# Attention with a threshold, then a mixture of experts: splitting tau - max behind its transposition

## The chip, the cores and the metric

The kernel runs on one core of one Trainium2 chip, in a single launch. The metric is the device time of that core in microseconds. In this document PE is TensorE's matmul row and PEld its weight loads, DVE is VectorE, ACT is ScalarE, POOL is GpSimd and SP is SyncE, whose queue issues most of the DMAs.

## The reference, cut to what matters

```python
# q, k, v: [8 batches, 8 heads, 576, 64] f32, tau = 0.02
scores = q @ k.T / 8
thresh = max(scores, axis=-1) - tau
scores = where(scores >= thresh, scores, -1e9)
attn   = exp(scores - max(scores)); attn /= sum(attn) + 1e-9
x = (attn @ v)                        # as [4608, 512]
# mixture of experts, top 1 of 8
logits = x @ w_gate; e = argmax(logits); gate = softmax(logits)[e]
out = gate * (relu(x @ w1[e]) @ w2[e])
```

Each row of scores keeps only the entries within tau of its maximum. The kernel must find the maximum first, and only then decide which entries live.

## The kernel before, in words

The 64 heads are taken as 32 pairs. For each pair n the scores are made twice. `s_unit` (L269) makes them with the queries on the partitions, ten units and a corner, and DVE reduces each unit to the negated maximum of its rows (L283, L288), into the tile `nm`: 128 partitions, nine tiles of queries, in two halves (the first 512 keys, the rest). Later `st_unit` (L334) makes them again with the keys on the partitions, ready for the product with v. There the maximum must be known for each column, that is for each query. It is brought in by the matmul itself: rows 64 to 66 of the operand `CQ` hold tau - max of each query, split in three f16 parts, and the same rows of `CK` hold ones, so that the second matmul of a unit (L341) adds tau - max to every score. After it ACT takes the exponential (L357), DVE sets what is below zero to nothing (`mask`, L360), ACT makes the f16 high part of the result (L365) and POOL the low part by a subtraction of two SBUF operands (L366). `av_piece` (L381) multiplies both with v.

`parts` (L290) is what turns `nm` into those three rows. On DVE it takes the smaller of the two negated maxima (L297), adds the threshold and rounds to f16 (L306), takes the remainder (L307), rounds that (L308) and takes what is left (L310). Each of the five works on 9 columns in SBUF and 128 partitions. Three steps later `turn` brings the 27 columns to 27 partitions with one f16 matmul against an identity (L321), ACT copies them from PSUM to SBUF (L326), and three DMAs on SP's queue write them to rows 64 to 66 of `CQ` (L328).

The order is written as steps: 11 steps a pair, in each of which one unit of `s` of a later pair and one of `st` of an earlier one are issued. The scores of pair n are finished 11 steps before its first `st` unit. Work that isn't a unit is put in a table by `plan` and `after` at a step and one of three places in it (FRONT, MID, END), and `chain` lays a list out at two operations a step, MID and END. A scheduler below that orders the instructions of each engine from this.

Between the units go the conversion of q, k and v (L206, L209, L242, L243), the normalisation of a finished batch, its gate (`logits`, `route`, `ranks`), and the scatter of its rows to a buffer by expert (`send`, L550). PSUM is eight banks: five for scores, two for the product with v, and one pool of one bank, `ps_m`, which `parts`, the gate's logits and its ranks share. When the last batch is scattered, the experts run: rows are gathered by expert, transposed by DMA, and go through two matrix products (L793, L820).

Of the kernel before, what the change touches and what calls it, by code (L numbers as in the profile page):

```python
# [9 lines left out]
F16 = mybir.dt.float16  # L10
F32 = mybir.dt.float32
I32 = mybir.dt.int32
U32 = mybir.dt.uint32
AF = mybir.ActivationFunctionType
ALU = mybir.AluOpType
AX = mybir.AxisListType

P = 128
B, H, S, D = 8, 8, 576, 64
# [23 lines left out]
CAP = NTOK  # L43

TUNE = dict(
    lead=10, cast=2, pst=3, sl=8, ll=15, sp0=3, sps=0, lv=-16, sv0=-6, sv1=2, av=2, g=4, l=3, d=4, g5=4, l5=3, d5=2, g6=1, l6=2, d6=2, g7=1, l7=1, d7=1, off=2, off5=1, off6=11, lg=4, lg7=13, km=16, rate=15, dh=1, do=3, ws0=6, wsd=1, w1d=5, plv=1, xv=3, so=0, sto=0, ord=0, sc=5, fa=3, fd=4, wa1=-70, wa2=-86, wl1=-28, wl2=-6, avb=2, route=1, ranks=7, pt2=1, pta=0, pch=0, pp=8, ew=4, maskat=0, w1a=-40, w1b=3,
)


# [1 line left out]
def kernel(  # L51
# [9 lines left out]
    nc = tc.nc  # L61

    cpool = ctx.enter_context(tc.tile_pool(name="cpool", bufs=1))
# [3 lines left out]
    ps_m = ctx.enter_context(tc.tile_pool(name="ps_m", bufs=1, space=bass.MemoryType.PSUM))  # L67
    small = ctx.enter_context(tc.tile_pool(name="small", bufs=3))
    rpool = ctx.enter_context(tc.tile_pool(name="rpool", bufs=1))
    tp = ctx.enter_context(tc.tile_pool(name="tp", bufs=1))  # L70
    ew = ctx.enter_context(tc.tile_pool(name="ew", bufs=4))
# [7 lines left out]
    op = apool.enter_context(tc.tile_pool(name="op", bufs=4))  # L79
    pp = apool.enter_context(tc.tile_pool(name="pp", bufs=8))  # L80


    ident = cpool.tile([P, P], F16, name="ident")
    make_identity(nc, ident)
    ones = cpool.tile([P, P], F16, name="ones")
    nc.gpsimd.memset(ones, 1.0)
# [4 lines left out]
    thr = cpool.tile([P, 1], F32, name="thr")  # L91
# [67 lines left out]
    st = {}  # L159
# [7 lines left out]
    FRONT, MID, END = range(3)  # L167

    def plan(k, f, where=END):
        assert (k, where) >= (now[0], slot[0])  # L170
        acts.setdefault(k, ([], [], []))[where].append(f)

    def after(k, f, where=END):
        plan(now[0] + k, f, where)

    def chain(k, fs):

        for i, f in enumerate(fs):
            i += slot[0] > FRONT and k == 0
            after(k + i // 2, f, END if i % 2 else MID)  # L180
# [108 lines left out]

    def parts(n):  # L290

        nm = st[n]["nm"]
        pt = small.tile([P, 3, 9], F16, tag="pt", name=f"pt_{n}")
        r1 = small.tile([P, 2, 9], F32, tag="r1", name=f"r1_{n}")
        r, x = r1[:, 0], r1[:, 1]
        v, a, g = nc.vector, nc.scalar, nc.gpsimd
        fs = [lambda: v.tensor_tensor(r, nm[:, 0], nm[:, 1], ALU.min)]  # L297
        if TUNE["pta"]:
            fs += [
                lambda: a.activation(pt[:, 0], r, AF.Identity, bias=thr),  # L300
                lambda: v.scalar_tensor_tensor(x, r, thr, pt[:, 0], ALU.add, ALU.subtract),
                lambda: a.copy(pt[:, 1], x),
            ]
        else:
            fs += [
                lambda: v.tensor_scalar(pt[:, 0], r, thr, None, ALU.add),  # L306
                lambda: v.scalar_tensor_tensor(x, r, thr, pt[:, 0], ALU.add, ALU.subtract),  # L307
                lambda: v.tensor_copy(pt[:, 1], x),  # L308
            ]
        fs.append(lambda: (g, v)[TUNE["pt2"]].tensor_tensor(pt[:, 2], x, pt[:, 1], ALU.subtract))  # L310
        if TUNE["pch"]:
            chain(0, fs)
            z = len(fs) // 2
        else:
            for f in fs:
                f()
            z = 0

        def turn():
            pst = ps_m.tile([P, 512], F32, tag="m", name=f"pst_{n}")  # L320
            nc.tensor.matmul(pst[0:27, 0:P], pt.rearrange("p a t -> p (a t)"), ident, start=True, stop=True)  # L321
            after(1, lambda: rows(pst), FRONT)

        def rows(pst):
            ptT = small.tile([27, P], F16, tag="ptT", name=f"ptT_{n}", bufs=2)
            nc.scalar.copy(ptT, pst[0:27, 0:P])  # L326
            for p in range(3):
                nc.sync.dma_start(  # L328
                    st[n]["CQ"][64 + p:65 + p].rearrange("p (t c) -> p t c", t=9), ptT[9 * p:9 * p + 9]
                )  # L330

        after(PST + z, turn)

    def st_unit(n, t):  # L334
        d = st[n]
# [39 lines left out]
    def x_tiles(b):  # L375
        if b not in xt:
            half = xt[b - 1][1] if b % 2 else xp.tile([P, H, W], F32, tag="xh", name=f"xh_{b}")
            xt[b] = (xp.tile([P, NT, H, W], F32, tag="x", name=f"x_{b}"), half)
        return xt[b]
# [49 lines left out]
    def finish(b):  # L429
        x = str(b) if b >= B - 3 else ""  # L430
        gap, lag, dist = (TUNE[z + x] for z in "gld")
        off = TUNE["off" + x] if b < B - 1 else 2
        n = NT + b % 2
        x4, xh = x_tiles(b)
        rs = small.tile([P, 5, H], F32, tag="rs", name=f"rs_{b}")
        eps = 1e-9 * SV / SX
        fs = [
            lambda: nc.vector.tensor_scalar(rs[:, 0:NT].unsqueeze(3), x4[:, :, :, D:W], eps, None, ALU.add),
            lambda: nc.vector.reciprocal(rs[:, 0:NT], rs[:, 0:NT]),
        ]  # L440
        if n > NT:
            fs += [
                lambda: nc.vector.tensor_scalar(rs[:, NT].unsqueeze(2), xh[:, :, D:W], eps, None, ALU.add),
                lambda: nc.vector.reciprocal(rs[:, NT], rs[:, NT]),
            ]
        chain(0, fs)
        xTs = {}

        def one(j):
            xr = x4[:, j] if j < NT else xh  # L450
            x = xp.tile([P, DM], F32, tag="xn", name=f"xn_{b}_{j}", bufs=2).rearrange("p (h d) -> p h d", h=H)
            eng = nc.vector if (b, j) in XV else nc.gpsimd
            eng.tensor_tensor(
                x, xr[:, :, 0:D], rs[:, j].unsqueeze(2).to_broadcast([P, H, D]), ALU.mult
            )
            x = x.rearrange("p (c u) d -> p c (u d)", c=4)
            Rv = R[:, j, 0:DM].bitcast(F16).rearrange("p (c h d) -> p c h d", c=4, h=2)

            def high():
                nc.scalar.copy(Rv[:, :, 0, :], x)  # L460
                eng.tensor_tensor(Rv[:, :, 1, :], x, Rv[:, :, 0, :], ALU.subtract)
                after(lag, turn)

            def turn():
                if j % 2 == 0:
                    xTs["t"] = rpool.tile([P, 2, 8, P], F16, tag="xT", name=f"xTg_{b}_{j}", bufs=3)
                xTs[j] = xT = xTs["t"][:, j % 2]
                nc.sync.dma_start_transpose(xT, R[:, j, 0:DM].bitcast(F16))

            after(lag, high)  # L470

        for j in range(n):
            after(off + gap * j, lambda j=j: one(j))
        after(off + gap * (n - 1) + 2 * lag + TUNE["lg7" if b == B - 1 else "lg"], lambda: logits(b, n, xTs, dist))

    def logits(b, n, xTs, dist):
        lg = ps_m.tile([P, 512], F32, tag="m", name=f"lg_{b}")
        lv = lg[:, 0:n * 2 * E].rearrange("p (j h e) -> p j h e", j=n, h=2)
        seq = [(0, 0)] + [(c, 1) for c in range(4)] + [(c, 0) for c in range(1, 4)]
        for j in range(n):  # L480
            for m, (c, h) in enumerate(seq):
                nc.tensor.matmul(
                    lv[:, j, 0:2 - h], xTs[j][:, 2 * c + h, :], wg[:, c, 0:2 - h, :],
                    start=(m == 0), stop=(m == 7),
                )
        after(1, lambda: nc.vector.tensor_reduce(
            L[:, 0:n, :], lv.rearrange("p j h e -> p j e h"), axis=AX.X, op=ALU.add
        ), FRONT)
        after(TUNE["route"], lambda: route(b, n, dist))
# [362 lines left out]
    NSTEP = len(st_order)  # L852
    av_order = [(a, i) for a in range(2) for i in range(NT)] + [(0, NT), (1, NT)]
    SL, LL = TUNE["sl"], TUNE["ll"]
    LEAD, CAST, PST = TUNE["lead"], TUNE["cast"], TUNE["pst"]
    KEND = NSTEP * NPAIR
    KM = KEND - TUNE["km"]
    NF = 3
# [146 lines left out]
    turn = [8]  # L1005
# [24 lines left out]
    if True:  # L1030
# [9 lines left out]
        while busy:  # L1040
# [3 lines left out]
            for z in (("st", "s"), ("s", "st"))[TUNE["ord"]]:  # L1044
                n, t = divmod(k + (NSTEP + LEAD if z == "s" else 0), NSTEP)
                if z == "s" and n < NPAIR:
                    s_unit(n, s_order[t])
                    if t == NSTEP - 1:
                        parts(n)
                elif z == "st" and 0 <= n < NPAIR:  # L1050
                    masks.append(st_unit(n, st_order[t]))
# [5 lines left out]
            n, t = divmod(k - TUNE["av"], NSTEP)  # L1057
# [94 lines left out]
```

## Time and profile before

| | |
|---|---|
| median of 3 runs | 1158.68 us (1156.25 to 1160.17) |
| the profiled execution | 1160.5 us, span 1158.5 us |
| PE busy | 970.1 us (84%) |
| DVE busy | 865.3 us (75%) |
| ACT busy | 645.4 us (56%) |
| POOL busy | 586.1 us (51%) |

The span runs from the first to the last instruction of the profiled execution. Busy shares over the whole span mix two stages: attention, to about 725 us, and the experts behind it. A row of the groups by line gives the busy time of all instructions of one line and shape, the mean of one, and how long the engine stood idle just before them.

### The profile page before, as it was taken

The numbers are of one execution on the slowest core, as the hardware profiler recorded it, in microseconds if no ns is written. First come the engines' busy times: TensorE is split into PE (matmuls) and PEld (weight loads), VectorE is DVE, ScalarE is ACT, GpSimd is POOL, SyncE is SP. The second block draws the span as 40 slices with busy tenths as digits, with TensorE's granted clock in tenths as the row PEclk, the third lists the DMA queues.
The fourth block names the chain that finished last, engine by engine and source line by source line (L and its number), as shares of the span: only waits on it lengthen the run. The fifth ranks groups of instructions, "written<-read, shape, count | busy, mean of one in ns | idle before, by whom it ended". The sixth has DMA issues, their size and how long they took to land. (4 is left out here: it accounts for less than half of the span.)

```text
span 1158.5 us, 26702 instructions
## 1 busy us (share of the span) xinstructions
PE 970.1 (84%) x10699; PEld 625.8 (54%) x10699; DVE 865.3 (75%) x1449; ACT 645.4 (56%) x998; POOL 586.1 (51%) x459
## 2 busy tenths in 40 slices
PE   4788788688778679778679768988799999999997
PEld 1354454355445345445346436765667667676774
DVE  8899999999999999999999997465242343234460
ACT  2667676677567667667567667342243344334451
POOL 2356764885585776676766686443312222222221
PEclk9889888999889989989989988989799999999999
DMA  6544433354344435345433442797974575666640
GB/s 190 133 139 105 116 75 96 118 115 110 87 115 125 123 82 138 93 108 137 127 62 89 119 116 66 227 246 225 221 220 144 157 208 148 164 200 163 227 135 25
DMA packets 142554, 159.06 MB, mean 137 GB/s; under 512 B 96345, under 2 KB 112731, under 8 KB 142428
## 3 DMA queue, kind: packets, MB, share of 16 engines
q1 hardware_dynamic: 133276, 127.88, 42.6%
q0 software_dynamic: 9152, 29.45, 7.8%
q8 instruction: 85, 1.39, 0.5%
q14 instruction: 41, 0.34, 0.1%
HBM read 90.24 MB, written 19.44 MB: 95 GB/s over the span
## 5 line engine op out<-in xcount | busy, mean ns | idle before, releaser
L366 POOL TENSOR_TENSOR pl<-e,ph 128x1024 f16<-128x1024 f32 x158 | 349.9, 2220 | 206.5 <-ACT ph L365 133.5
L357 ACT ACTIVATE e<-st,ntau 128x512 f32<-128x512 f32 (+1 forms) x352 | 221.4, 651 | 67.7 <-PE st L341 63.7
L360 DVE SCALAR_TENSOR_TENSOR e<-st,e 128x512 f32<-128x512 f32 (+1 forms) x352 | 217.6, 635 | 6.4 <-ACT e L357 6.3
L288 DVE TENSOR_REDUCE nm<-s 128x1 f32<-128x512 f32 x320 | 199.8, 633 | 16.6 <-PE s L278 15.1
L793 PEld LDWEIGHTS <-wb 128*128 128x128 f16 x2304 | 193.6, 100 | 30.8 <-DMA xTm<-R 11.7
L365 ACT CAST ph<-e 128x1024 f16<-128x1024 f32 x160 | 166.7, 1042 | 74.8 <-DVE e L360 74.1
L276 PE MATMUL s<-QK 128*128 128x512 f16 (+3 forms) x640 | 146.9, 306 | 72.5 <-DVE nm L288 41.9
L793 PE MATMUL h<-xTm,wb 128*128 128x256 f16 (+2 forms) x2112 | 197.9, 256 | 11.2 <-DMA xTm<-R 11.2
L820 PE MATMUL y<-wb,hl 128*128 128x512 f16 (+1 forms) x1056 | 203.3, 362 | 3.2 <-ACT hl L781 2.4
L340 PE MATMUL st<-QK 128*128 128x512 f16 (+3 forms) x640 | 147.0, 309 | 61.7 <-DVE nm L288 34.5
L405 PE MATMUL av<-vop,ph 128*128 128x64 f16 (+1 forms) x1280 | 168.6, 200 | 0.0
L407 PE MATMUL av<-vop,ph 128*128 128x65 f16 (+1 forms) x1280 | 168.6, 201 | 0.0
L406 PE MATMUL av<-vop,pl 128*128 128x65 f16 (+1 forms) x1280 | 168.2, 200 | 0.4 <-POOL pl L366 0.4
L712 DVE SCALAR_TENSOR_TENSOR wb<-wf,wb 128x1024 f16<-128x1024 f32 x96 | 121.5, 1301 | 42.6 <-ACT wb L711 41.1
L820 PEld LDWEIGHTS <-hl 128*128 128x128 f16 (+1 forms) x1056 | 94.5, 100 | 103.0 <-issue 4.2
L341 PE MATMUL st<-CQ,ck 128*128 128x512 f16 (+3 forms) x640 | 145.0, 306 | 5.0 <-DMA CQ<-ptT 5.0
L278 PE MATMUL s<-ck,CQ 128*128 128x512 f16 (+3 forms) x640 | 145.9, 303 | 0.0
L406 PEld LDWEIGHTS <-pl 128*128 128x128 f16 (+1 forms) x1280 | 126.9, 105 | 26.7 <-issue 12.9
L407 PEld LDWEIGHTS <-ph 128*128 128x128 f16 (+1 forms) x1280 | 126.8, 105 | 25.0 <-issue 14.2
L405 PEld LDWEIGHTS <-ph 128*128 128x128 f16 (+1 forms) x1280 | 126.9, 105 | 21.6 <-issue 12.2
L751 DVE COPY gt<-R 128x1 f32<-128x1 f32 x35 | 5.4, 154 | 148.3 <-DMA out_dram<-o,gt 127.5
L781 ACT ACTIVATE hl<-h 128x512 f16<-128x512 f32 (+1 forms) x80 | 45.6, 572 | 126.0 <-PE h L793 126.0
(184 smaller groups left out, 1338.4 us busy)
## 6 DMA issues: line engine op xcount, KB each, us to landing
wf<-in_w_dram SPq DMA_DIRECT2D x96, 512.0 KB
qkf<-in_qk_dram SPq DMA_DIRECT2D x32, 576.0 KB
vf<-in_v_dram SPq DMA_DIRECT2D x16, 640.0 KB
QK<-hi SPq DMA_DIRECT2D x64, 144.0 KB
QK<-hi SPq DMA_DIRECT2D x64, 72.0 KB
QK<-lo SPq DMA_DIRECT2D x64, 72.0 KB
ck<-lo SPq DMA_DIRECT2D x64, 72.0 KB
CQ<-hi SPq DMA_DIRECT2D x64, 64.0 KB
```

The lines of the kernel that those rows point to most:

```text
L276: nc.tensor.matmul(sc[rows, oc], d["QA"][a][:, cols], d["KB"][a][:, CH[c]], start=True, stop=False)
L288: nc.vector.tensor_reduce(o, sc[:, 0:width(t)], axis=AX.X, op=ALU.max, negate=True)
L340: nc.tensor.matmul(sc[rows, oc], d["KB"][a][:, cols], d["QA"][a][:, CH[c]], start=True, stop=False)
L357: nc.scalar.activation(pf, sc, AF.Exp, bias=ntau, scale=0.125 / SS)
L360: nc.vector.scalar_tensor_tensor(pf, sc, 0.0, pf, ALU.is_ge, ALU.mult)
L365: nc.scalar.copy(h, pd)
L366: (nc.vector if (n, t) in PLV else nc.gpsimd).tensor_tensor(l, pd, h, ALU.subtract)
L405: nc.tensor.matmul(av[rows, a, 0:D], h, vop[:, tv, W:W + D], start=False, stop=False)
L406: nc.tensor.matmul(av[rows, a], l, vop[:, tv, 0:W], start=False, stop=False)
L407: nc.tensor.matmul(av[rows, a], h, vop[:, tv, 0:W], start=False, stop=a == 1 and i >= 2 and j == NT - 1)
L793: nc.tensor.matmul(o, Wt[:, c, wh, f], x, start=c == 0 and z == 0, stop=c == 3 and z == 2,)
L820: nc.tensor.matmul(o, h[:, hh], Wt[:, f, wh, c], start=f == 0 and z == 0, stop=f == 7 and z == 2)
```

## The change

The five operations on 128 partitions become one: a reduction over the two halves of `nm` into one f32 tile of 9 columns. That tile is transposed as f32, one step later, by a matmul with an f32 identity into the bank of `ps_m`. The split is then made on 9 partitions and 128 columns: ACT reads PSUM, adds the threshold and rounds to f16; DVE writes the remainder to other columns of the same bank; ACT rounds that; DVE subtracts. The four are put by `chain` on two steps. Then the three DMAs are issued. The SBUF tile of the three parts has one buffer instead of two, and the options of `TUNE` for the old split go (`pst`, `pt2`, `pta`, `pch`).

```diff
-    ident = cpool.tile([P, P], F16, name="ident")
+    ident = cpool.tile([P, P], F32, name="ident")
...
-        fs = [lambda: v.tensor_tensor(r, nm[:, 0], nm[:, 1], ALU.min)]
...
-                lambda: v.tensor_scalar(pt[:, 0], r, thr, None, ALU.add),
-                lambda: v.scalar_tensor_tensor(x, r, thr, pt[:, 0], ALU.add, ALU.subtract),
-                lambda: v.tensor_copy(pt[:, 1], x),
...
-        fs.append(lambda: (g, v)[TUNE["pt2"]].tensor_tensor(pt[:, 2], x, pt[:, 1], ALU.subtract))
...
+        r = small.tile([P, 9], F32, tag="r", name=f"r_{n}")
+        nc.vector.tensor_reduce(r, nm.rearrange("p a t -> p t a"), axis=AX.X, op=ALU.min)
         def turn():
-            pst = ps_m.tile([P, 512], F32, tag="m", name=f"pst_{n}")
-            nc.tensor.matmul(pst[0:27, 0:P], pt.rearrange("p a t -> p (a t)"), ident, start=True, stop=True)
-            after(1, lambda: rows(pst), FRONT)
+            ps = ps_m.tile([P, 512], F32, tag="m", name=f"pst_{n}")
+            nc.tensor.transpose(ps[0:9, 0:P], r, ident)
+            x, y = ps[0:9, 0:P], ps[0:9, P:2 * P]
+            t = small.tile([9, 3, P], F16, tag="ptT", name=f"ptT_{n}", bufs=1)
+            v, a = nc.vector, nc.scalar
+            chain(1, [
+                lambda: a.activation(t[:, 0], x, AF.Identity, bias=thr[0:9]),
+                lambda: v.scalar_tensor_tensor(y, x, thr[0:9], t[:, 0], ALU.add, ALU.subtract),
+                lambda: a.copy(t[:, 1], y),
+                lambda: (v.tensor_tensor(t[:, 2], y, t[:, 1], ALU.subtract), rows(t)),
+            ])
-        def rows(pst):
-            ptT = small.tile([27, P], F16, tag="ptT", name=f"ptT_{n}", bufs=2)
-            nc.scalar.copy(ptT, pst[0:27, 0:P])
+        def rows(t):
             for p in range(3):
                 nc.sync.dma_start(
-                    st[n]["CQ"][64 + p:65 + p].rearrange("p (t c) -> p t c", t=9), ptT[9 * p:9 * p + 9]
+                    st[n]["CQ"][64 + p:65 + p].rearrange("p (t c) -> p t c", t=9), t[:, p]
                 )
-        after(PST + z, turn)
+        after(1, turn)
...
-        rs = small.tile([P, 5, H], F32, tag="rs", name=f"rs_{b}")
+        rs = small.tile([P, 5, H], F32, tag="rs", name=f"rs_{b}", bufs=2)
```

## Rows read from the trace of the kernel before

**Rows 1.** Busy time by stretches: us, each engine's busy time (instructions), clock, DMA share, GB/s

```profile
202.90:219.50 16.60, 14.51 (x168) 7.87 (x166) 16.60 (x38) 13.76 (x24) 13.67 (x10) 1.00 0.56 167
50.00:100.00 50.00, 42.83 (x579) 25.90 (x577) 49.55 (x77) 37.92 (x59) 31.16 (x16) 0.93 0.50 136
100.00:700.00 600.00, 468.77 (x6111) 282.98 (x6107) 582.23 (x939) 407.44 (x665) 411.06 (x252) 0.92 0.42 106
28.00:725.00 697.00, 550.98 (x7200) 332.70 (x7199) 668.01 (x1092) 476.40 (x775) 465.09 (x285) 0.91 0.43 108
```

**Rows 2.** Waits of 100 to 700 us: total us, times, longest us

```profile
PE s L276 <- DVE nm L288: 39.2, 39, 5.9
...
ACT ptT L326 <- PE pst L321: 18.1, 9, 4.6
...
DVE nm L288 <- PE s L278: 11.9, 20, 1.7
```

**Rows 3.** Groups by line, DVE, the lines of `parts`: busy us, mean ns, idle before

```profile
L306 DVE TENSOR_SCALAR pt<-r,thr 128x9 f16<-128x9 f32 x32 | 53.4, 1668 | 0.1
...
L297 DVE TENSOR_TENSOR r<-nm 128x9 f32<-128x9 f32 x32 | 27.2, 852 | 0.1
L308 DVE CAST pt<-r 128x9 f16<-128x9 f32 x32 | 22.2, 695 | 0.1
...
L307 DVE SCALAR_TENSOR_TENSOR r<-r,thr,pt 128x9 f32<-128x9 f32 x32 | 18.3, 571 | 0.0
L310 DVE TENSOR_TENSOR pt<-r,pt 128x9 f16<-128x9 f32 x32 | 17.8, 556 | 0.0
```

**Rows 4.** Single lines of DVE: shortest/median/longest ns, first and last start, forms

```profile
L297 DVE TENSOR_TENSOR r<-nm x32: 152/424/5042, 27.9 to 693.4; 128x9 f32<-128x9 f32 x32
...
L310 DVE TENSOR_TENSOR pt<-r,pt x32: 154/158/2117, 35.0 to 699.6; 128x9 f16<-128x9 f32 x32
...
L288 DVE TENSOR_REDUCE nm<-s x320: 208/677/695, 18.1 to 691.9; 128x1 f32<-128x512 f32 x160
...
L360 DVE SCALAR_TENSOR_TENSOR e<-st,e x352: 206/677/693, 42.2 to 722.2; 128x512 f32<-128x512 f32 x156, 128x64 f32<-128x64 f32 x20
...
L533 DVE TENSOR_TENSOR ps<-rk,base_e x8: 175/182/193, 197.5 to 767.1; 128x32 f32<-128x32 f32 x4, 128x40 f32<-128x40 f32 x4
...
L538 DVE TENSOR_REDUCE pos<-ps x8: 169/175/196, 202.9 to 767.5; 128x4 f32<-128x32 f32 x4, 128x5 f32<-128x40 f32 x4
```

**Rows 5.** Timeline of one stall, DVE and POOL: start us, us, instruction

```profile
333.39 7.48 DVE L306 TENSOR_SCALAR pt<-r,thr 128x9 f16<-128x9 f32 x1
333.44 2.14 POOL L366 TENSOR_TENSOR pl<-e,ph 128x1024 f16<-128x1024 f32 x1
335.54 1.15 POOL L461 TENSOR_TENSOR R<-xn,R 128x512 f16<-128x512 f32 x1
336.64 4.19 POOL L366 TENSOR_TENSOR pl<-e,ph 128x1024 f16<-128x1024 f32 x2
```

**Rows 6.** Groups by line and shape, PE

```profile
L341 PE MATMUL st<-CQ,ck 128*128 128x512 f16 x256 | 100.1, 395 | 5.0 <-DMA CQ<-ptT 5.0
...
L321 PE MATMUL pst<-ident,pt 128*27 128x128 f16 x32 | 7.5, 235 | 17.5 <-DVE pt L310 17.2 <-ACT ptT L326 0.3
```

**Rows 7.** Groups by line, DVE, other operations on SBUF alone

```profile
L209 DVE SCALAR_TENSOR_TENSOR lo<-qkf,hi 128x1152 f16<-128x1152 f32 (+1 forms) x33 | 57.4, 1742 | 1.1 <-ACT hi L206 1.1
...
L243 DVE SCALAR_TENSOR_TENSOR vop<-vf,vop 128x640 f16<-128x640 f32 x32 | 30.7, 958 | 0.5 <-ACT vop L242 0.5
...
L511 DVE TENSOR_TENSOR w<-L,mx 128x32 f32<-128x32 f32 (+1 forms) x8 | 8.8, 1100 | 0.1
...
L519 DVE TENSOR_TENSOR oh<-w,mw 128x32 f16<-128x32 f32 (+1 forms) x8 | 4.6, 573 | 0.0
```

**Rows 8.** The chain that ended last, its beginning: start us, us, what

```profile
800.88 0.97 DMA xs<-R,posi
...
808.69 9.06 DMA xTm<-R
817.74 0.05 issue
817.79 8.38 PE h L793 x96
```

More of the change, by code (lines that the diff above doesn't have):

```diff
@@ L45 @@
 TUNE = dict(
-    lead=10, cast=2, pst=3, sl=8, ll=15, sp0=3, sps=0, lv=-16, sv0=-6, sv1=2, av=2, g=4, l=3, d=4, g5=4, l5=3, d5=2, g6=1, l6=2, d6=2, g7=1, l7=1, d7=1, off=2, off5=1, off6=11, lg=4, lg7=13, km=16, rate=15, dh=1, do=3, ws0=6, wsd=1, w1d=5, plv=1, xv=3, so=0, sto=0, ord=0, sc=5, fa=3, fd=4, wa1=-70, wa2=-86, wl1=-28, wl2=-6, avb=2, route=1, ranks=7, pt2=1, pta=0, pch=0, pp=8, ew=4, maskat=0, w1a=-40, w1b=3,
+    lead=10, cast=2, sl=8, ll=15, sp0=3, sps=0, lv=-16, sv0=-6, sv1=2, av=2, g=4, l=3, d=4, g5=4, l5=3, d5=2, g6=1, l6=2, d6=2, g7=1, l7=1, d7=1, off=2, off5=1, off6=11, lg=4, lg7=13, km=16, rate=15, dh=1, do=3, ws0=6, wsd=1, w1d=5, plv=1, xv=3, so=0, sto=0, ord=0, sc=5, fa=3, fd=4, wa1=-70, wa2=-86, wl1=-28, wl2=-6, avb=2, route=1, ranks=7, pp=8, ew=4, maskat=0, w1a=-40, w1b=3,
 )
@@ L292, in parts @@
         nm = st[n]["nm"]
[L293 to L296, printed above, removed]
-        fs = [lambda: v.tensor_tensor(r, nm[:, 0], nm[:, 1], ALU.min)]
-        if TUNE["pta"]:
-            fs += [
-                lambda: a.activation(pt[:, 0], r, AF.Identity, bias=thr),
-                lambda: v.scalar_tensor_tensor(x, r, thr, pt[:, 0], ALU.add, ALU.subtract),
[L302 to L305, printed above, removed]
-                lambda: v.tensor_scalar(pt[:, 0], r, thr, None, ALU.add),
-                lambda: v.scalar_tensor_tensor(x, r, thr, pt[:, 0], ALU.add, ALU.subtract),
-                lambda: v.tensor_copy(pt[:, 1], x),
-            ]
@@ L310, in parts @@
-        fs.append(lambda: (g, v)[TUNE["pt2"]].tensor_tensor(pt[:, 2], x, pt[:, 1], ALU.subtract))
[L311 to L317, printed above, removed]
-        def turn():
-            pst = ps_m.tile([P, 512], F32, tag="m", name=f"pst_{n}")
-            nc.tensor.matmul(pst[0:27, 0:P], pt.rearrange("p a t -> p (a t)"), ident, start=True, stop=True)
-            after(1, lambda: rows(pst), FRONT)
@@ L854 @@
     SL, LL = TUNE["sl"], TUNE["ll"]
-    LEAD, CAST, PST = TUNE["lead"], TUNE["cast"], TUNE["pst"]
+    LEAD, CAST = TUNE["lead"], TUNE["cast"]
     KEND = NSTEP * NPAIR
```

## The prediction

> **What bounds the kernel now.** I read the busy time by stretches first, because the kernel has two stages with different limits. [...] PE stands idle 131 us of the 600, DVE 18.
>
> What does DVE spend it on? The groups by line show five lines of `parts` that are far too dear for 9 columns: 53.4, 27.2, 22.2, 18.3 and 17.8 us for 32 instructions each, 138.9 us together [rows 3]. The spread tells why: the shortest of them take 152 to 222 ns (sum of the five shortest 0.891 us), the longest of the two shown 5.0 and 2.1 us (the first and the last of the five stand in [rows 4]). The reader is to see that the instructions next to them in the same engine don't spread: the reductions and masks that read PSUM lie between 206 and 695 ns over 672 instances, and so does a two-input operation with one operand in PSUM (175 to 193), and a reduction with SBUF on both sides (169 to 196) [rows 4]. What stretches is an operation with SBUF operands alone that is not a reduction.
>
> The timeline shows on what it waits. L306 starts at 333.39 and ends at 340.87; POOL starts a subtraction at 333.44, runs three further ones without a gap, and ends the last at 340.83 [rows 5]. DVE stood until POOL's backlog had run dry. In those 7.4 us no mask was made and no maximum, so PE and ACT ran out as well. Such an operation costs the whole pipeline, not DVE alone.
>
> **The change part by part.** What goes from DVE: five operations per pair, 32 pairs, 138.9 us. Without the stalls they would be 32 x 0.891 = 28.5 us; the stalls are 110.4.
>
> What comes to DVE: one reduction of 18 columns to 9 with SBUF on both sides, 0.175 (L538 in [rows 4]); one three-operand operation on 128 columns with PSUM in and out; one subtraction on 128 columns with one operand in PSUM. For the second I take L360's two shapes: 206 ns at 64 columns, 677 at 512, so 1.05 ns a column, and 0.273 us at 128. For the third, L533's 182 ns at 32 to 40 columns plus some 90 columns gives 0.275. Sum 0.723 x 32 = 23.1 us. Against the 28.5 that is 5 us less, and I count it as nothing, since successive DVE records overlap a little and two more instructions' overlap goes.
>
> Do the new operations stall? Two of them have an operand in PSUM; the third is a reduction, and the eight of L538 go up to 196 ns. Bounds: nothing, or 0.69 us each as now (110.4/160), 66 us for 96. I take nothing, because the rows for PSUM operands never show a stall in 672 instances.
>
> [...]
>
> What comes to ACT: one copy of 27 rows and 128 columns goes (0.25 us), two activations of 9 rows and the same columns come; 0.25 x 32 = 8 us more on an engine that is 68% busy. Covered by its idle time; if ACT became the bound, it would be those 8 us.
>
> What comes to PE: the transposition moves the same 128 columns, now f32. The trace holds no f32 matmul. Bounds: as now, 0.235; or the time of 512 columns, 0.395 [rows 6]. The second costs 5 us over 32, inside PE's 131 us of idle time. I take nothing and keep 5 as the far end.
>
> The three row transfers per pair stay on SP's queue and keep their size. They now wait for DVE's last subtraction instead of ACT's copy, one step of the order earlier than before. Behind them in SP's queue are the transfers that build the next pairs' operands. The consumer is eight steps away, so I cost this at nothing.
>
> The wait that is new: the chain is PE, ACT, DVE, ACT, DVE, four hand-overs, where it was DVE, PE, ACT. Behind DVE's two waiting operations stand the maxima and masks, for which PE waits; behind ACT's second one stand the exponentials. The bank (the only one of that pool) is held until the last subtraction, and the gate's matmuls and ranks queue for it on PE, 8 batches. Each of the chain's operations is put behind a mask or an exponential of its step, which is what hides the hand-over. This is the ground of the slow rival.
>
> **What is late next.** Taking 110 us out of 697 needs PE to do its work in less. Two things give some of it back.
>
> First, DVE will wait for PE. Between 202.9 and 219.5 one pair took 16.60 us with DVE busy throughout, PE busy 14.51 and the clock at 1.00 [rows 1], against the 21.5 us that a pair takes on average ((693.4 - 27.9)/31, first and last start of L297 in [rows 4]). So the other work allows that pace, but with PE at 87% there is little slack. Lower bound of the loss 0, upper 62 (the rival below). I take 18, as much again as DVE's idle time today.
>
> Second, other DVE operations on SBUF alone remain: L209 57.4 us, L243 30.7, and six lines of the routing that sum to 35.4 for 48 instructions ([rows 7], of the six the first and the last). At 1.05 ns a column their unstalled times are 43.3, 26.0 and about 8.6, so about 46 us of stall is in them. POOL's share rises from 69% to some 81% (411 of about 510), and the stalls with it: 8 us by proportion, 46 if they double. I take 10.
>
> Sum: 110 - 18 - 10 = 82 us. The stage behind is bound by a chain that begins with the last scatter at 800.88, the gather's transposition at 808.69 and then PE without a gap [rows 8]; it hangs on the end of attention and moves as a whole, so nothing of the 82 is lost there. The profiled execution took 1160.5 us (span 1158.5); 1160.5 - 82 = 1078.5. The median of the runs is 1158.68, 1.8 lower, so 1077.
>
> **The rivals.**
>
> A, nothing is given back: 1160.5 - 110 = 1050. For it speaks the 16.6 us pair; against it that PE has 131 us of idle time in all, most of it just these stalls.
>
> B, PE becomes the bound. Its highest share in a 50 us stretch of this stage is 42.83 (86%) at a clock of 0.93 [rows 1]. If it can't pass that, 550.98 + 5 us of PE work need 649 us instead of 697: 48 us less, 1112. If the clock stays at 1.00 as in the 16.6 us pair, it doesn't bind. The forecast lies between A and B.
>
> C, the other side: the four hand-overs. ACT's copy waited for PE's transposition 9 times, 18.1 us, 2.0 each, up to 4.6 [rows 2]. If both of DVE's waits in a chain cost that, it is 4.0 x 32 = 128 us on the bounding engine, more than the 110: 1160.5 + 18 = 1178. It decides above 1.7 us a wait (110/64). Against it: DVE is the engine that lags in this stage, so what it waits for is mostly done.
>
> D, the change doesn't do what it says: the stall goes to any short DVE operation, wherever its operands lie. Then 66 us stay, and the run takes 1160.5 - 44 = 1116. The 672 unstalled instances speak against it. [...]
>
> **How the numbers follow.** Forecast (1060 to 1098) 0.50, A 0.15, B 0.23, D 0.03, C 0.06, and 0.03 for a C that just cancels the gain. A measurement of this kernel tells about 0.3% from no change. Forecast, A, B and D are faster: 0.91. Same 0.03, slower 0.06. The range reaches from 1045 (A with the 5 us that I left out) to 1122 (B and D inside), which leaves out C and the tails. Predicted 1077.
>
> **What would show it.** The five lines of `parts` on DVE give way to three of about 0.72 us a pair with no instance over 0.4 us; a pair takes 18 to 19 us instead of 21.5; DVE's share in the stage falls below 95% and PE's rises above 84%; the mean of L209 or of the routing's operations rises by a tenth to a quarter; from the last scatter to the end the time stays. It would be wrong if PSUM operations show durations of microseconds (D), if DVE shows idle time before the new operations, ended by ACT, of over 1 us a pair (C), or if the stage's PE share stops at 86% with PE's own waits gone (B).

## The result, and the profile after

The changed kernel takes 1109.69 us (median of 4 runs, 1107.99 to 1111.50). Beside it the kernel before took 1157.57. The ratio is 0.9584, 95% interval 0.9559 to 0.9609: 48 us faster. I had predicted 1077 with a range of 1045 to 1122. The sign and the mechanism held; of the 82 us forecast, 48 came. The profiled execution took 1107.99 us (span 1105.5).

First the lines of the split in the groups by line of DVE, after. They answer to [rows 3].

```profile
L305 DVE SCALAR_TENSOR_TENSOR pst<-pst,thr,ptT 9x128 f32<-9x128 f32 x32 | 10.8, 338 | 0.0
L307 DVE TENSOR_TENSOR ptT<-pst,ptT 9x128 f16<-9x128 f32 x32 | 8.5, 267 | 1.2 <-ACT ptT L306 1.2
L295 DVE TENSOR_REDUCE r<-nm 128x9 f32<-128x18 f32 x32 | 5.2, 161 | 0.2
```

24.5 us where 138.9 stood. And none of the three spreads any more; shortest, median and longest in ns, against up to 5042 in [rows 4]:

```profile
L305 DVE SCALAR_TENSOR_TENSOR pst<-pst,thr,ptT x32: 337/337/341, 32.2 to 645.1; 9x128 f32<-9x128 f32 x32
L307 DVE TENSOR_TENSOR ptT<-pst,ptT x32: 216/269/279, 33.8 to 646.6; 9x128 f16<-9x128 f32 x32
L295 DVE TENSOR_REDUCE r<-nm x32: 151/159/175, 27.8 to 637.5; 128x9 f32<-128x18 f32 x32
```

So 114 us of DVE's time in the split went, and the kernel got 48 us faster. Where is the rest? Two views show it. The busy time by stretches from 28 us to the end of the last masks (us, then PE, PEld, DVE, ACT, POOL, the granted clock, DMA); before:

```profile
28.00:723.00 695.00, 548.98 (x7156) 330.70 (x7155) 667.32 (x1091) 474.55 (x772) 463.09 (x285) 0.91 0.43 108
```

and after:

```profile
28.00:674.00 646.00, 530.77 (x7142) 322.53 (x7142) 598.71 (x1040) 476.43 (x805) 459.85 (x286) 0.93 0.46 117
```

The attention stage is 49 us shorter, which is nearly all of the span's 53. In it DVE is busy 68.6 us less, not 114, and idle 47.3 us instead of 27.7, 19.6 more. So its other operations grew by 45.8 us in this stage. DVE's share fell from 96% to 93%, PE's rose from 79% to 82%.

The DVE time that did not go is in other operations, whose code the change does not touch. The groups by line of after, which answer to [rows 7] (L498 and L499 are the routing's two copies, L514 and L515 before):

```profile
L209 DVE SCALAR_TENSOR_TENSOR lo<-qkf,hi 128x1152 f16<-128x1152 f32 (+1 forms) x33 | 67.4, 2044 | 14.0 <-ACT hi L206 13.4 <-DMA CQ<-hi 0.4
L243 DVE SCALAR_TENSOR_TENSOR vop<-vf,vop 128x640 f16<-128x640 f32 x32 | 36.9, 1155 | 0.6 <-ACT vop L242 0.6
...
L499 DVE COPY R<-tid 128x4 int32<-128x4 int32 (+1 forms) x8 | 18.4, 2306 | 1.5 <-DMA xs<-R,posi 1.5
...
L498 DVE COPY was<-run 128x8 f16<-128x8 f16 x8 | 5.1, 633 | 0.0
```

The same copies before:

```profile
L515 DVE COPY R<-tid 128x4 int32<-128x4 int32 (+1 forms) x8 | 3.6, 453 | 6.9 <-DMA xs<-R,posi 6.8
L514 DVE COPY was<-run 128x8 f16<-128x8 f16 x8 | 3.2, 405 | 0.0
```

L209 costs 10.0 us more, L243 6.2, the two copies 16.7: 32.9 us on 81 instructions of the same shapes. Over the whole span DVE's busy time went from 865.3 to 793.7; by the split alone it would be 750.9, so 42.8 us net came to other operations, and these four lines are three quarters of it. One line's figure comes from one profiled execution and is rough: in e5 below, where DVE does the same work as in the changed kernel, L209 takes 62.9 us, L243 33.7 and the token copy 23.7 instead of 18.4.

That these are the same stalls is seen in the timeline of after: start, us, instruction, and in brackets the idle time before it and what ended it.

```profile
305.64 4.21 POOL L350 TENSOR_TENSOR pl<-e,ph 128x1024 f16<-128x1024 f32 x2
306.55 4.52 DVE L209 SCALAR_TENSOR_TENSOR lo<-qkf,hi 128x1152 f16<-128x1152 f32 x1 [2.22 <-ACT hi L206]
310.01 1.94 POOL L534 DMA_INDIRECT xs<-R,posi  x1 [0.17 <-issue]
311.00 0.68 DVE L288 TENSOR_REDUCE nm<-s 128x1 f32<-128x512 f32 x1
311.72 0.58 PE L324 MATMUL st<-QK 128*128 128x512 f16 x1 [5.66 <-DVE nm L288]
```

L209 starts while POOL works through two subtractions, which end at 309.85. The shortest of its shape takes 1.335 us (1.341 before), and this one ends at 311.07, 1.22 us after POOL. PE waits 5.66 us for the maximum behind it. It is the picture of [rows 5] with another victim.

[rows 5] and this one are not the usual case, though. Take as a stall every DVE instruction of the attention stage that is more than 0.3 us longer than the shortest of its line and shape, and its length over that shortest one as the time lost. Before there are 105, with 167.9 us lost, 108.7 of it on the five lines of the split; after there are 56, with 99.4 us. Take the shortest length off the end of a stall, and 103 of the 105, and all of the 56, come to within 0.2 us of the end of a POOL operation. This says more plainly than the spread that it is POOL that DVE waits for. But in 96 of the 105 DVE waited only for the operation that POOL had under way, and in 34 of these POOL's next one followed within 0.1 us and didn't hold DVE. So it goes in this stretch of the kernel before, POOL first, then DVE's three operations on SBUF:

```profile
133.93 2.14 POOL L366 TENSOR_TENSOR pl<-e,ph 128x1024 f16<-128x1024 f32 x1
136.02 1.17 POOL L461 TENSOR_TENSOR R<-xn,R 128x512 f16<-128x512 f32 x1
137.15 1.05 POOL L453 TENSOR_TENSOR xn<-x,rs 128x512 f32<-128x512 f32 x1
138.15 2.13 POOL L366 TENSOR_TENSOR pl<-e,ph 128x1024 f16<-128x1024 f32 x1
...
135.12 0.98 DVE L306 TENSOR_SCALAR pt<-r,thr 128x9 f16<-128x9 f32 x1
136.61 0.61 DVE L307 SCALAR_TENSOR_TENSOR r<-r,thr,pt 128x9 f32<-128x9 f32 x1
137.74 0.48 DVE L308 CAST pt<-r 128x9 f16<-128x9 f32 x1
```

L306 ends at 136.10, L307 at 137.22, L308 at 138.22: each 0.02 to 0.03 us after the POOL operation under way, with POOL's next one already running. Only 9 of the 105 (44.8 us) and 12 of the 56 (44.1 us) went on through two to six of POOL's operations.

### The profile page after: what moved, and what is told of

It reads as the page before. It is cut to its first block, busy times and chain, and to the rows that moved or that the text cites. A ratio compares the mean times of both kernels' runs of the same rounds, so it can differ in the third digit from the quotient of the medians.

```text
span 1105.5 us, 26826 instructions
## 1 busy us (share of the span) xinstructions
PE 950.0 (86%) x10699; PEld 616.1 (56%) x10699; DVE 793.7 (72%) x1385; ACT 646.7 (59%) x1030; POOL 574.5 (52%) x459
## 4 chain that ended last, share of the span: by engine, by line
PE 45%; DVE 26%; DMA 11%; issue 10%; ACT 4%; POOL 2%; SPq 2%; POOLq 0%; DVEq 0%; ACTq 0%
PE h L777 15%; PE y L804 13%; DVE nm L288 7%; DVE e L344 6%; PE st L324 3%; PE s L276 3%; DVE lo L209 3%; PE st L325 3%; PE s L278 2%; DMA out_dram<-o,gt 2%; DVE vop L243 2%; DMA xs<-R,posi 2%; DMA CQ<-hi 2%; PE av L390 2%; PE av L391 1%
## 5 line engine op out<-in xcount | busy, mean ns | idle before, releaser
L350 POOL TENSOR_TENSOR pl<-e,ph 128x1024 f16<-128x1024 f32 x158 | 344.4, 2184 | 167.4 <-ACT ph L349 128.5
L341 ACT ACTIVATE e<-st,ntau 128x512 f32<-128x512 f32 (+1 forms) x352 | 218.9, 647 | 37.7 <-PE st L325 35.3
L288 DVE TENSOR_REDUCE nm<-s 128x1 f32<-128x512 f32 x320 | 199.1, 630 | 19.7 <-PE s L278 18.4
L276 PE MATMUL s<-QK 128*128 128x512 f16 (+3 forms) x640 | 145.3, 305 | 67.0 <-DVE nm L288 37.8
L390 PE MATMUL av<-vop,pl 128*128 128x65 f16 (+1 forms) x1280 | 161.8, 197 | 3.2 <-POOL pl L350 3.1
L389 PE MATMUL av<-vop,ph 128*128 128x64 f16 (+1 forms) x1280 | 161.5, 197 | 0.6 <-ACT ph L349 0.6
L391 PE MATMUL av<-vop,ph 128*128 128x65 f16 (+1 forms) x1280 | 161.9, 197 | 0.0
L390 PEld LDWEIGHTS <-pl 128*128 128x128 f16 (+1 forms) x1280 | 123.0, 102 | 26.1 <-issue 8.5
L391 PEld LDWEIGHTS <-ph 128*128 128x128 f16 (+1 forms) x1280 | 123.2, 102 | 23.2 <-issue 10.8
L389 PEld LDWEIGHTS <-ph 128*128 128x128 f16 (+1 forms) x1280 | 123.6, 102 | 22.1 <-issue 10.5
L816 POOL DMA_INDIRECT out_dram<-o,gt x40 | 44.8, 1120 | 142.7 <-ACT o L815 123.5
```

Of the source, the lines that this page charges most:

```text
L276: nc.tensor.matmul(sc[rows, oc], d["QA"][a][:, cols], d["KB"][a][:, CH[c]], start=True, stop=False)
L288: nc.vector.tensor_reduce(o, sc[:, 0:width(t)], axis=AX.X, op=ALU.max, negate=True)
L341: nc.scalar.activation(pf, sc, AF.Exp, bias=ntau, scale=0.125 / SS)
L350: (nc.vector if (n, t) in PLV else nc.gpsimd).tensor_tensor(l, pd, h, ALU.subtract)
L389: nc.tensor.matmul(av[rows, a, 0:D], h, vop[:, tv, W:W + D], start=False, stop=False)
L390: nc.tensor.matmul(av[rows, a], l, vop[:, tv, 0:W], start=False, stop=False)
```

## The experiments

Two theories are set against each other, with variants. L: a DVE operation whose operands all lie in SBUF (reductions excepted) stands while POOL runs operations that read SBUF; the change takes five such operations a pair away, and the stalls pass partly to those that remain. Against it: H, the old order is slow by itself; P, it is the 9 partitions or the smaller number of operations; B, PE became the bound and took the rest. All ratios are to the kernel before, on the same chip.

**Without POOL's subtraction: the kernel before (e1) and the changed one (e2).** The same edit in both:

```diff
-            (nc.vector if (n, t) in PLV else nc.gpsimd).tensor_tensor(l, pd, h, ALU.subtract)
...
-            d["Ph"][t], d["Pl"][t] = h, l
+            d["Ph"][t], d["Pl"][t] = h, h
...
-            d["Ph"][t], d["Pl"][t] = h[:, j], l[:, j]
+            d["Ph"][t], d["Pl"][t] = h[:, j], h[:, j]
```

> The kernel before, without POOL's subtraction for the low part (the product with v reads the high part twice, so PE's work is the same): left out is the low part of the exponentials. Theory L (an operation of DVE whose operands all lie in SBUF stands while POOL runs an operation that reads SBUF): the five lines of the split fall from 138.9 us to 30 to 45, and the time to 1030 to 1060 us. Theory H (the old order is slow by itself: more instructions of DVE on the path, transposition three steps later): the five lines may shrink, but this run stays about 48 us, 4%, above the same edit of the changed kernel.

> The changed kernel with the same edit: left out is the low part of the exponentials. Theory L: within 1.5% of e1_before_no_low, as nothing is left for the change to save but some 5 us of DVE; L209 falls from a mean of 2044 ns to 1350 or so. Theory H: 4% faster than e1_before_no_low.

Measured: e1 1053.30 us, ratio 0.9101 (0.9069 to 0.9132); e2 1059.56, ratio 0.9153 (0.9123 to 0.9182). The split in e1, groups by line of DVE:

```profile
L306 DVE TENSOR_SCALAR pt<-r,thr 128x9 f16<-128x9 f32 x32 | 8.2, 257 | 0.5
L308 DVE CAST pt<-r 128x9 f16<-128x9 f32 x32 | 7.9, 245 | 0.1
L307 DVE SCALAR_TENSOR_TENSOR r<-r,thr,pt 128x9 f32<-128x9 f32 x32 | 7.4, 230 | 0.0
L297 DVE TENSOR_TENSOR r<-nm 128x9 f32<-128x9 f32 x32 | 6.6, 207 | 0.2
L310 DVE TENSOR_TENSOR pt<-r,pt 128x9 f16<-128x9 f32 x32 | 5.2, 161 | 0.0
```

The same five instructions of the same code take 35.3 us instead of 138.9. And L209 in e2 is back at its bare length:

```profile
L209 DVE SCALAR_TENSOR_TENSOR lo<-qkf,hi 128x1152 f16<-128x1152 f32 (+1 forms) x33 | 44.0, 1337 | 31.2 <-ACT hi L206 31.1
```

With POOL out of the way the change saves nothing; it is about 6 us slower, at the edge of what the intervals tell apart. H falls: these runs show nothing wrong with the old order. The small difference the other way is of the size of what the four hand-overs may cost (e2 has 5.4 us of DVE waiting in front of the new three-operand operation, by the groups by line), but no run isolates it.

**The split in PSUM, but on 128 partitions and ahead of the transposition (e3).** The kernel before, with

```diff
-        r, x = r1[:, 0], r1[:, 1]
-        fs = [lambda: v.tensor_tensor(r, nm[:, 0], nm[:, 1], ALU.min)]
+        pst = ps_m.tile([P, 512], F32, tag="m", name=f"pst_{n}")
+        r, x = pst[:, 128:137], pst[:, 144:153]
+        v.tensor_reduce(r, nm.rearrange("p a t -> p t a"), axis=AX.X, op=ALU.min)
...
-        after(PST + z, turn)
+        after(1, turn)
```

and the other four operations as they were, all on DVE.

> The kernel before, with the split still ahead of the transposition and on 128 partitions and 9 columns, all five operations on DVE, but its f32 intermediates in PSUM (in the bank that the transposition uses) and the minimum made by a reduction; the transposition one step later instead of three. Theory L: the five lines take 28 to 40 us in all, none over 0.5 us, and the time is that of the changed kernel, 1110 us, within 1.5%. Theory P (it is the 9 partitions or the fewer DVE operations that help): 1140 us or more. Theory H (the transposition's later place): not separated from L by this run alone.

Measured: 1112.15 us, ratio 0.9606 (0.9555 to 0.9657), which holds the changed kernel's. Single lines of DVE in e3, shortest, median, longest ns:

```profile
L297 DVE TENSOR_REDUCE pst<-nm x32: 161/168/174, 28.0 to 643.8; 128x9 f32<-128x18 f32 x32
L298 DVE TENSOR_SCALAR pt<-pst,thr x32: 183/219/230, 31.8 to 644.6; 128x9 f16<-128x9 f32 x32
L299 DVE SCALAR_TENSOR_TENSOR pst<-pst,thr,pt x32: 215/222/235, 33.7 to 646.3; 128x9 f32<-128x9 f32 x32
L300 DVE CAST pt<-pst x32: 151/157/171, 34.6 to 647.3; 128x9 f16<-128x9 f32 x32
L301 DVE TENSOR_TENSOR pt<-pst,pt x32: 150/156/170, 34.8 to 648.2; 128x9 f16<-128x9 f32 x32
```

Still five operations, 128 partitions, 9 columns, no ACT, no f32 transposition and the old buffer counts: none over 0.235 us, 29.5 us together. P falls. The whole gain of the change is to be had by writing the intermediates to PSUM and making the minimum by a reduction. (The transposition was also put earlier here; e1 against e2 gives no sign that this order is worth anything by itself, but with POOL's subtraction in place no run shows it alone.)

**Behind the transposition, but in SBUF (e4).** The changed kernel, with

```diff
+            xs9 = tp.tile([9, 2, P], F32, tag="ge", name=f"xs9_{n}")
+            z, y = xs9[:, 0], xs9[:, 1]
...
-                lambda: a.activation(t[:, 0], x, AF.Identity, bias=thr[0:9]),
-                lambda: v.scalar_tensor_tensor(y, x, thr[0:9], t[:, 0], ALU.add, ALU.subtract),
+                lambda: (a.activation(t[:, 0], x, AF.Identity, bias=thr[0:9]), a.copy(z, x)),
+                lambda: v.scalar_tensor_tensor(y, z, thr[0:9], t[:, 0], ALU.add, ALU.subtract),
```

> The changed kernel, split behind the transposition on 9 partitions, but with its f32 intermediates copied to and kept in SBUF (one more ACT copy a pair, 8 us of ACT in all). Theory L: the two DVE operations of the chain show instances of over 1 us and sum to 50 to 90 us instead of 19.3; the time is 1120 to 1145. Theory P: they stay below 0.4 us each, and the time is 1108 to 1118.

Measured: 1137.74 us, ratio 0.9829 (0.9798 to 0.9859). The two DVE operations of the chain:

```profile
L307 DVE SCALAR_TENSOR_TENSOR xs<-xs,thr,ptT x32: 329/560/7772, 32.5 to 677.1; 9x128 f32<-9x128 f32 x32
L309 DVE TENSOR_TENSOR ptT<-xs,ptT x32: 269/402/5696, 34.1 to 680.3; 9x128 f16<-9x128 f32 x32
```

The shortest are near what they were (329 against 337, 269 against 216), the longest are 7.8 and 5.7 us. They sum to 77.0 us against 19.3. Two operations a pair put back into SBUF give back more than half of the gain (with one more copy on ACT a pair, 7.6 us in all). e3 and e4 together are L's case: the place of the operands decides, not the partitions and not the order.

**Less work for PE (e5), less for DVE (e6).** From the changed kernel; e5 leaves out one of the three products with v, e6 the DVE operation that makes the low part of v.

```diff
# e5
-            nc.tensor.matmul(av[rows, a, 0:D], h, vop[:, tv, W:W + D], start=False, stop=False)
# e6
-        after(1, lambda: nc.vector.scalar_tensor_tensor(
-            vop[:, u, :, D + 1:2 * D + 1], vf[:, u], SV, vop[:, u, :, 0:D], ALU.mult, ALU.subtract
-        ))
```

> The changed kernel without the product of the high part with the low part of v (1280 matmuls of 64 columns fewer of PE; left out is the low part of v; DVE still makes it). Some 38 us of PE's work at 30 ns each. Theory L (behind the change DVE is still the bound of the attention stage, its stalls have moved to its other operations on SBUF): less than 12 us faster than the changed kernel's 1109.7. Rival B (PE is the bound now and gave the gain back): 25 us faster or more.

> The changed kernel without DVE's operation that makes the low part of v (L243, 32 instances, 36.9 us with their stalls, 26 without; left out is the low part of v, which stays zero; PE still multiplies with it). Theory L: 18 to 37 us faster than the changed kernel (1073 to 1092). Rival B: less than 10 us faster.

Measured: e5 1110.10 us, ratio 0.9562 (0.9531 to 0.9593), the same as the changed kernel within the intervals. e6 1092.23, ratio 0.9439 (0.9371 to 0.9508), about 17 us faster. The busy time from 100 to 600 us, after and then e5:

```profile
100.00:600.00 500.00, 420.21 (x5745) 255.69 (x5744) 471.13 (x812) 376.79 (x640) 369.78 (x229) 0.95 0.47 117
```

```profile
100.00:600.00 500.00, 397.88 (x4703) 224.04 (x4703) 464.65 (x805) 377.00 (x638) 368.53 (x228) 0.92 0.46 115
```

PE is busy 22 us less in 500 and simply stands longer; DVE's share is 94% and then 93%. The granted clock fell from 0.95 to 0.92, and in the kernel before one of L276's matmuls of 512 columns took 0.38 us where the clock was 1.00 (at 203.03 us) and 0.62 where it was 0.50 (at 343.57); so some of PE's cut was taken back, and e5 is not a pure cut. But B, which asked for 25 us, is out. DVE is still the bound: 36.9 us off it gave 17, a little less than the low end that I had expected (18). What it lost in stalls came back: L243 had 10.9 us of the 99.4 lost in the changed kernel's attention stage, and without it 100.9 us are lost there.

**The routing's copies on ACT: from the changed kernel (e7), from e3 (e8).**

```diff
-            lambda: nc.vector.tensor_copy(was, run),
+            lambda: nc.scalar.copy(was, run),
-            lambda: nc.vector.tensor_copy(
+            lambda: nc.scalar.copy(
                 R[:, 0:n, DM + 1:DM + 2], tid[:, b // 2, 4 * (b % 2):4 * (b % 2) + n].unsqueeze(2)
             ),
```

> The changed kernel with the two small copies of the routing (the running count and the token numbers, L498 and L499, 8 of each, 23.5 us on DVE, of which some 21 are stall) on ACT instead of DVE. Theory L: 8 to 20 us faster than the changed kernel (1090 to 1102), as part of the stalls moves on to DVE's next operations on SBUF. Rival B: within 5 us of it.

> The kernel of e3_before_psum128 with the same two copies on ACT (there 31.2 us on DVE). Theory L: 10 to 25 us faster than e3 (1087 to 1102). Rival B: within 5 us of e3.

Measured: e7 1107.12 us, ratio 0.9528 (0.9497 to 0.9559); e8 1099.26, ratio 0.9461 (0.9425 to 0.9496). By the ratios e7 gains about 6 us on the changed kernel, less than the 8 to 20 expected, with intervals that just touch; e8 gains 17 on e3, as expected. In e7, groups by line of DVE (the profiled execution was the slowest of e7's four, 1114.58 us):

```profile
L209 DVE SCALAR_TENSOR_TENSOR lo<-qkf,hi 128x1152 f16<-128x1152 f32 (+1 forms) x33 | 72.9, 2213 | 10.7 <-ACT hi L206 9.7 <-DMA CQ<-hi 0.7
L243 DVE SCALAR_TENSOR_TENSOR vop<-vf,vop 128x640 f16<-128x640 f32 x32 | 43.9, 1373 | 0.9 <-ACT vop L242 0.9
```

23.5 us of copies went from DVE, and 12.5 came back on these two lines. The sum is firmer than the lines: the copies had 20.9 us of the 99.4 lost in stalls, and without them 94.2 are lost. In e8 the sum falls from e3's 109.3 to 95.8.

**From e8: the low part of v on POOL (e9), four more routing operations off DVE (e10).**

```diff
# e9
-        after(1, lambda: nc.vector.scalar_tensor_tensor(
-            vop[:, u, :, D + 1:2 * D + 1], vf[:, u], SV, vop[:, u, :, 0:D], ALU.mult, ALU.subtract
+        nc.scalar.activation(vf[:, u], vf[:, u], AF.Copy, scale=SV)
+        after(1, lambda: nc.gpsimd.tensor_tensor(
+            vop[:, u, :, D + 1:2 * D + 1], vf[:, u], vop[:, u, :, 0:D], ALU.subtract
# e10
-            lambda: tt(w, w, rank8.unsqueeze(1).to_broadcast(bc), ALU.mult),
+            lambda: nc.gpsimd.tensor_tensor(w, w, rank8.unsqueeze(1).to_broadcast(bc), ALU.mult),
-            lambda: tt(run, run, got, ALU.add),
+            lambda: nc.gpsimd.tensor_tensor(run, run, got, ALU.add),
-                lambda: tt(ps, ps, oh, ALU.mult),
+                lambda: nc.gpsimd.tensor_tensor(ps, ps, oh, ALU.mult),
-                lambda: nc.vector.tensor_copy(posi[:, 0:n].unsqueeze(2), pos),
+                lambda: nc.scalar.copy(posi[:, 0:n].unsqueeze(2), pos),
```

> The kernel of e8_psum128_copies with DVE's operation for the low part of v moved to POOL (ACT scales v first, then POOL subtracts; one more ACT operation of 0.75 us a pair). DVE loses 39.6 us of work, 14 of it stall; POOL gains some 1.3 us a pair. Theory L: 8 to 20 us faster than e8 (1079 to 1091), as in e6, less what POOL's longer backlog adds to L209 and the routing. Against it, if POOL gets near its bound: slower than e8.

> The kernel of e8_psum128_copies with four more of the routing's small operations off DVE (three products and sums of SBUF operands on POOL, one cast on ACT; 8 of each; 24 us on DVE there, 19 of it stall). If stalls simply go with the operations that have them: 10 us or more faster than e8. If they move on to the operations that remain (L209, L243 and the rest of the routing), as the totals of e7 and e8 suggest: within 6 us of e8, with L209's mean above e8's 2.3 us.

Measured: e9 1091.38 us, ratio 0.9431 (0.9374 to 0.9488); e10 1087.36, ratio 0.9401 (0.9340 to 0.9462). Both lie below e8, by some 3 and 7 us by the ratios, but their intervals overlap e8's, so neither step is shown to gain. e9's expectation of 8 us or more was not met. e10's two theories asked for 10 or more and for less than 6; its 7 lies between them, and only the mean of L209 above 2.3 us came as the second one had it (the four operations take 22.4 us in e8, not the 24 that I had read):

```profile
L209 DVE SCALAR_TENSOR_TENSOR lo<-qkf,hi 128x1152 f16<-128x1152 f32 (+1 forms) x33 | 88.6, 2687 | 11.5 <-ACT hi L206 11.4
```

L209's mean is 1742 ns before, 2044 after the change, 2213 in e7, 2326 in e8 and 2687 in e10, and 1337 when POOL doesn't subtract (e2). But it is 1910 in e3, 1907 in e5, and 2126 in e9, where one more victim is gone than in e8. So one line does not show that each victim taken away makes the next one dearer. The time lost in stalls over the attention stage is the better measure: 167.9 us before, 99.4 after, 109.3 in e3, 95.0 in e5, 100.9 in e6, 94.2 in e7, 95.8 in e8, 71.8 in e9, 86.0 in e10. Against the changed kernel, what e6 took away came back whole and what e7 took away to three quarters; against e8, e9 and e10 have 24.0 and 9.8 us less.

In e9 that gained next to nothing, because DVE no longer fills the stage. From 100 to 600 us, e8 and then e9:

```profile
100.00:600.00 500.00, 423.79 (x5828) 259.41 (x5827) 474.18 (x860) 379.61 (x630) 383.94 (x232) 0.95 0.48 119
```

```profile
100.00:600.00 500.00, 429.14 (x5821) 259.21 (x5820) 436.33 (x838) 391.56 (x656) 405.12 (x257) 0.95 0.47 119
```

DVE's share falls from 95% to 87%, PE's is 86%, POOL's 81%; what the stage waits for there, no run isolates. e8, e9 and e10 beat both kernels clear of their intervals; e10 is the fastest, 6% below the kernel before.

## Why the prediction was right, and where its size was off

- **What bounds, and why the five lines are dear**: right. Before, DVE's share of the attention stage was 96% and PE's 79%. e1, e3 and e4 show from three sides why the lines are dear, and so do the lengths of the split's operations: the new reduction takes up to 175 ns, e3's up to 174, the forms with an operand in PSUM up to 341, the forms on SBUF up to 8109 (L306 before). In 96 of the 105 stalls before DVE waited for one POOL operation. In the other 9, as in [rows 5], it waited through two to six in a row. So the prediction's sentence that DVE stood until POOL's backlog had run dry holds for the stall that it read, and not for most.
- **What goes and what comes on DVE**: 138.9 against 24.5 us, forecast 23.1. By the sum it is 114 us off the split, where the forecast went on with the 110 of the stalls. The three-operand operation on PSUM took 0.338 us where L360's rows gave 0.273; the subtraction 0.267 (0.275), the reduction 0.161 (0.175).
- **No stall on the new operations**: right; the longest is 0.341 us.
- **What the change costs where hardly a stall is left**: in e1 and e2, where 26 and 5 us are left of the stalls, the change is some 6 us slower, at the edge of the intervals.
- **PE's f32 transposition**: 0.280 us against 0.235, between the bounds (0.235 and 0.395), and hardly waited for (1.2 us by ACT in all).
- **DVE waits more for PE and ACT**: taken as 18 us; DVE's idle time in the stage grew by 19.6. The 18 stood on no row but DVE's idle time of before, taken once more, so that it came so near is luck.
- **The stalls of the remaining operations on SBUF**: this is the term that was mis-sized. I took 10 us, by the proportion of POOL's share, with a far end of 46. The operations outside the split grew by 45.8 us in the stage, 42.8 over the span. Two things were wrong in it. First, what was there already: I counted 46 us of stalls in L209, L243 and six lines of the routing; all operations outside the split lost 59.2 us in 40 stalls. The routing's two copies (6.8 us before) were not in my sum, and 16.7 us of the growth came on them. Second, how it grows: POOL's share of the stage went from 67% to 71%, and the time lost outside the split from 59.2 to 99.4 us, in 56 stalls instead of 40, and of 1.8 us each instead of 1.5. So of the 108.7 us that the split had lost, 40 came back elsewhere. e6 and e7 show the same: of the 10.9 us of stalls that e6 took away all came back, of e7's 20.9 three quarters. Why they pass on, and why e9's did not, is not shown.
- **The sum**: on DVE 114.4 us less for the split, 45.8 more for the rest, 19.6 more idle time; 49 us, by which the stage is shorter. This is bookkeeping (busy and idle time make up the stage) and shows where the time went, not why.
- **The stage behind moves as a whole**: nearly; 53.0 us of the span against 49 in attention, so some 4 us came behind it. The last scatter starts at 800.9 us before and at 757.1 after, 43.8 earlier, and from it to the end the time was to stay and fell by 9 us; no run says why.
- **The range held, the forecast's own bracket did not**: 1109.7 lies above 1060 to 1098, on which the prediction had put 0.50, and next to the times of rivals B (1112) and D (1116), for which the range had been left wide. The time alone could not have ruled those two out. **B** is out by e5: with 22 us in 500 less for PE nothing changed, and PE's share is 82%, below the 86% that it should have stopped at. **D** is out by the new operations, none of which took over 0.341 us. **C** asked for idle time of DVE of over 1 us a pair before them: it is 0.0 us in all before L305 and 1.2 before L307; ACT waits for DVE instead, 21.2 us before L306. **A** is out by both terms above.
- **What should have shown**: a pair takes (637.5 - 27.8)/31 = 19.7 us, not 18 to 19; PE's share is 82%, not above 84%; L209's mean rose by 17% as said, but L499's by a factor of five.

## What to carry to other kernels

When short DVE operations show durations of microseconds, sort them by where their operands lie, not by their size. Here an intermediate in PSUM, and a reduction in place of a two-input minimum, took the split out of POOL's way at no price of their own: e3's five lines take 29.5 us, where the old five would take 28.5 at their shortest. But count on getting only part of the stall back. Of 109 us that the split had lost, 40 came back on other operations on SBUF, among them two small copies that my sum had left out: list every such operation before you price the rest, and don't price it in proportion to POOL's share. A run with POOL's work left out says how much there is to gain at most (here 104 us for the kernel before, in which is also what else waits for POOL), and whether an edit does more than dodge POOL.

## What the runs showed of the hardware that I had not expected

- Most DVE operations that have to wait for POOL wait for the operation under way and get in before POOL's next one, even where that follows at once (34 of 105 before). A few wait through several: 9 of 105 before, up to 8.11 us through six, and 12 of 56 after, up to 8.43 us through six. All of the 9 lie within 3 us of an indirect DMA of POOL, against 18 of the other 96; after, 10 of the 12 against 13 of the other 44. What makes them wait longer is not shown.
- The stalls pass on in part. 23.5 us of copies taken off DVE in e7 came back as 12.5 us on two other lines, and the time lost in stalls fell by 5 us only; in e9 what was taken away stayed away, and the time hardly fell.
- An activation on 9 rows of 128 columns from PSUM with a bias per partition took 0.350 us on ACT (median 0.354), a plain copy of the same size 0.246.
